# Layer two's output products of five column pairs by Strassen's scheme, with weights streamed from DRAM

## The chip, the cores and the metric

One core of a Trainium2 chip. The metric is device time of one execution in microseconds (us); of several runs the median is given.

## The reference, cut to what is computed

Attention over channels gives a 6016 x 256 matrix, and two layers follow, each a product with a 256 x 2048 matrix, an activation, and a product with a 2048 x 256 matrix. The change touches layer two and the preparation of its weights.

```python
def _moe2_ref(x, w_in, w_out) -> np.ndarray:
    h = x @ w_in
    g = np.maximum(0.01 * h, h)
    return (g @ w_out).astype(np.float32)

def reference(**kwargs):
    ...
    attn_out = _attn_ref(**attn_kwargs)
    B, S, D = attn_out.shape
    x = attn_out.reshape(B * S, D)
    x = _moe_ref(x=x, **moe_kwargs)
    return _moe2_ref(x=x, **moe2_kwargs)
```

## The kernel before

Activations are kept transposed: features on the 128 partitions, tokens along the free axis. The 6016 tokens are taken in six pairs `p` of two blocks `u`, 512 tokens each (448 in the last pair). The 2048 hidden features are taken in eight steps `f`; a step handles feature tiles `f` and `f + 8`. So one step of one pair is, on either side of the activation, a 2 x 2 block product: first weights (2 x 2 tiles of 128 x 128) times inputs (2 x 2 tiles of 128 x 512), then output weights times activated tiles.

Each fp32 product is made of three fp32r matmuls, from a high part and a low part of each operand: high by high, low by high, high by low (`terms`, the helper whose line L92 issues nearly all matmuls). A "product" below is three matmuls of 512 columns. The high part is a cast on ScalarE, the low part a subtraction on VectorE (`halves`, or the two written apart).

In every pair but the very first of layer one, the first 2 x 2 product goes by Strassen's scheme in the Winograd form: seven products instead of eight, in the blocks A11, S2, A12, S3, S1, S4, A22 of combined weights and with the combined inputs B11, T2, B21, T3, T1, B22, T4. `step` issues them into two PSUM banks, h0 (`pa`) and h1 (`pb`). Copies and additions on ScalarE and VectorE between the products, and accumulation on top of what a bank already holds, form the four hidden tiles. The second 2 x 2 product is done plainly: eight products, summed over the steps in the four banks y00, y01, y10, y11 (`put`). So a step is 15 products, 45 matmuls.

The output products of a step lag by about a step. They stand in a list, and `step` takes some of them between its own products, so that TensorE has two products to do while a bank is read by another engine. Two such turnarounds recur. After product S1 into `pa`, VectorE adds it to `tt`, and only then may S4 accumulate into `pa`. After S4, VectorE adds `pa` to `tv`, and only then may the next step's A11 start in `pa`. Engines run their own instructions in the order of the program text; nothing is reordered by a scheduler.

Layer two's weights are prepared in layer one, by a generator `jobs` that `step` advances with `go_on(count)`, a few VectorE instructions at a time: a float64 word is turned to fp32, for the first weights the combined blocks are formed, and high and low parts are stored in DRAM (`w2a`, `w2o`). In layer one's last pair each step reloads weights of layer two, once, into the tiles `wa` and `wo` that layer one no longer needs; there they stay for all of layer two. `prefetch` loads the next pair's inputs and forms their combinations between the products; `switch` forms those that must wait until the pair ends.

Of the kernel before, what the change touches and what calls it, by code (L numbers as in the profile page):

```python
# [7 lines left out]
F32 = mybir.dt.float32  # L8
# [9 lines left out]
def tile_kernel(  # L18
# [28 lines left out]
    nc = tc.nc  # L47
# [35 lines left out]
    w2o = [dram.tile([P, 2, 2, C], F32, name=f"w2o{f}") for f in range(NF)]  # L83
# [30 lines left out]
    with tc.manual_schedule():  # L114
# [26 lines left out]
        def load_piece(key):  # L141
# [3 lines left out]
            if name in ("wi", "w2i"):  # L145
# [55 lines left out]
        def convert(key):  # L201
# [43 lines left out]
            if name == "w2o":  # L245
                w = early.tile([P, 2, BLK], F32R, tag="ws", name="w2o", bufs=2)
                nc.vector.tensor_copy(w[:, 0], flat)
                yield
                subtract(w[:, 1], flat, w[:, 0].bitcast(F32))
                nc.sync.dma_start(  # L250
                    out=w2o[f].rearrange("p h s c -> p h (s c)"), in_=w.bitcast(F32)
                )
                stored.add(key)
                yield
                return
            hi, lo = (
                early.tile([P, 7, P], F32R, tag="ws", name=f"w2a{x}", bufs=2) for x in "hl"
# [4 lines left out]
            yield  # L262
            yield from combine(a)
            nc.vector.tensor_copy(hi[:, 3:], a)
            yield
            subtract(lo[:, 3:], a, hi[:, 3:].bitcast(F32))
            for i, x in enumerate((hi, lo)):
                nc.sync.dma_start(out=w2a[f][:, i], in_=x.bitcast(F32))
# [385 lines left out]
        ys, left = {}, {}  # L654

        def put(item, kc):
# [4 lines left out]
            if key not in ys:  # L661
# [5 lines left out]
            c0 = slice(kc * P, (kc + 1) * P)  # L667
            terms(ys[key][kc][:, :w], (wo[g][:, 0, s, c0], wo[g][:, 1, s, c0]),
                  (gh, gl), first, final)
# [22 lines left out]
        def finish(layer, p, u, kc, y):  # L692
# [10 lines left out]
            if kc == 0:  # L703
                outs[p, u] = early.tile([P, KC, BLK], F32, tag="cv", name="o", bufs=3)
            o = outs[p, u]
            nc.vector.transpose(out=o[:, kc, :w], in_=y)  # L706
            for a in range(P // SB):

                (nc.scalar if p == NPAIR - 1 and a % 2 else nc.sync).dma_start(
                    out=blocks_of(out, p, u, kc, a), in_=blocks_in(o[:, kc, :], p, a)  # L710
                )
# [65 lines left out]
        def reload(f):  # L777

            while ("w2i", f) not in stored:
                go_on(1)  # L780
            pool = early if f < EARLY else late
            wa[f] = pool.tile([P, 2, 7, P], F32R, tag=f"wa{f}", name=f"wa2{f}")
            nc.sync.dma_start(out=wa[f].bitcast(F32), in_=w2a[f])

        def reload_out(f):
            while ("w2o", f) not in stored:
                go_on(1)
            pool = early if f < EARLY else late
            wo[f] = pool.tile([P, 2, 2, C], F32R, tag=f"wo{f}", name=f"wo2{f}")
            nc.sync.dma_start(out=wo[f].bitcast(F32), in_=w2o[f])  # L790
# [69 lines left out]

        def step(layer, p, f):
# [3 lines left out]
            x = xa[p % 2 if layer == 1 else (NPAIR + p) % 2]  # L865
            wf = wa[f]

            def product(dst, a, xs, b, more=False):
                terms(dst, (wf[:, 0, a], wf[:, 1, a]), (xs[:, 0, b, :w], xs[:, 1, b, :w]),
                      not more, True, more)  # L870

            pa, pb = (bank(f"h{i}")[:, :w] for i in range(2))

            def kept(tag):
                return early.tile([P, BLK], F32, tag=tag, name=tag)[:, :w]

            def outputs(count):
                for _ in range(min(count, len(slots))):
                    put(*slots.pop(0))

            tp, tv, tt = (kept(tag) for tag in ("tp", "tv", "tt"))
            product(pa, A11, x, B11)
            nc.scalar.copy(pb, pa)  # L883
            finish_step()
            slots = [(item, kc) for item in pend for kc in range(KC)]
            pend.clear()
            outputs(2)
            product(pb, S2, x, T2, more=True)
            nc.scalar.copy(tv, pb)  # L889
            product(pa, A12, xbt, B21, more=True)  # L890
            act(layer, tp, pa)
            outputs(1)
            product(pb, S3, x, T3, more=True)
            nc.scalar.copy(tt, pb)  # L894
            product(pa, S1, x, T1)
# [9 lines left out]
            outputs(len(slots) - 3)  # L905
            cc = late.tile([P, 2, BLK], F32, tag="cc", name="cc")[:, :, :w]
            product(pa, S4, xbt, B22, more=True)
            add(cc[:, 0], tv, pa)
            product(pb, A22, xbt, T4, more=True)
# [3 lines left out]
            if f:  # L913
                go_on(2)
            fetch()
# [3 lines left out]
            begun.append((layer, p, f, cc))  # L919
            if f < NF - 1:  # L920
                go_on(3)
            fetch()

        def last_step(layer, p, f):
# [3 lines left out]
            x = xa[p % 2 if layer == 1 else (NPAIR + p) % 2]  # L928
            wf = wa[f]

            def product(dst, a, xs, b, more=False):
                terms(dst, (wf[:, 0, a], wf[:, 1, a]), (xs[:, 0, b, :w], xs[:, 1, b, :w]),
                      not more, True, more)
# [7 lines left out]
            nc.scalar.copy(tp, pa)  # L941
            product(pb, S2, x, T2)
            add(tv, tp, pb)
            product(pc, S1, x, T1)
            add(tt, tv, pc)
            product(pd, S3, x, T3)
            add(tt, tt, pd)
# [98 lines left out]
```

## Time and profile before

| | us |
|---|---|
| median of 3 runs | 1036.0 |
| lowest and highest | 1035.88, 1036.09 |
| the profiled execution, its own time | 1036.65 |
| its span, first to last instruction | 1034.9 |
| TensorE (PE) busy | 1027.8 (99%) |
| VectorE (DVE) busy | 625.4 (60%) |
| ScalarE (ACT) busy | 677.0 (65%) |
| granted TensorE clock, share of full | 0.999 |

PEld is TensorE's weight load, which lies beside the matmuls. SP is the engine that issues nearly all DMAs. "Idle before" is the time that an engine stood still just ahead of a group of instructions, and the name behind the arrow is what ended it. A matmul's duration in the trace contains the tail of a pipeline, so the time that one takes from the engine is read from the starts of two groups, not from a duration.

### The profile page before, as it was taken

To read this page: it belongs to the slowest core of one execution; us is meant where nothing else is said; L and a number is where in the kernel's file an instruction comes from. 1 tells how busy PE (TensorE), PEld (TensorE's weight loads), DVE (VectorE), ACT (ScalarE), POOL (GpSimd) and SP (SyncE) were. 2 spreads that over 40 slices of the span, in tenths; PEclk is the share of its full clock that TensorE was granted. 3 is DMA by queue.
4 is the path that set the end of the run, shared out by engine and by line. 5 is a ranking of instruction groups with operands and counts; after the bars stand their busy time and mean duration, and the time that the engine had idled before them with its cause. 6 is when DMAs were issued, how large, how long until landed. Compare 5 with 4: busy or idle time off the path is not lost.

```text
span 1034.9 us, 12664 instructions
## 1 busy us (share of the span) xinstructions
PE 1027.8 (99%) x4664; PEld 868.1 (84%) x4664; DVE 625.4 (60%) x991; ACT 677.0 (65%) x1135; POOL 0.8 (0%) x7
## 2 busy tenths in 40 slices
PE   9999999999999999999999999999999999999998
PEld 7888878888888888888998888888888888888997
DVE  7899865667676767666654445455345455444434
ACT  7675556676676667667666666666666667566664
POOL 0000000000000000000000000000000000000000
PEclk9999999999999999999999999999999999999999
DMA  9765413015125114223644003002101200300202
GB/s 351 249 163 152 134 42 92 10 31 148 56 72 148 69 67 127 85 77 130 238 161 153 1 1 81 2 1 38 43 1 23 60 1 4 74 1 1 42 1 36
DMA packets 124862, 81.83 MB, mean 79 GB/s; under 512 B 97664, under 2 KB 108928, under 8 KB 123520
## 3 DMA queue, kind: packets, MB, share of 16 engines
q1 hardware_dynamic: 120512, 80.04, 26.1%
q10 hardware_dynamic: 4288, 0.98, 0.4%
q8 instruction: 36, 0.59, 0.2%
q14 instruction: 26, 0.21, 0.1%
HBM read 55.05 MB, written 25.95 MB: 78 GB/s over the span
## 4 chain that ended last, share of the span: by engine, by line
PE 98%; DMA 1%; DVE 0%; ACTq 0%; issue 0%; SPq 0%; DVEq 0%
PE y L92 50%; PE h L92 44%; PE y L406 3%; DMA qk<-in_k_dram 1%; PE h L553 1%; PE y L553 0%; ACTq L339 0%; PE y L511 0%; PE h L426 0%; DVE tt L99 0%; DVE o L706 0%; PE h L535 0%; PE h L500 0%; SPq L339 0%; DVEq L99 0%
## 5 line engine op out<-in xcount | busy, mean ns | idle before, releaser
L92 PE MATMUL y<-gd,wo 128*128 128x512 f32 (+1 forms) x1248 | 310.5, 386 | 0.0
L92 PE MATMUL h<-xa,wa 128*128 128x512 f32 (+1 forms) x1152 | 304.6, 386 | 0.0
L92 PE MATMUL y<-g,wo 128*128 128x512 f32 (+1 forms) x1044 | 275.0, 385 | 0.0
L92 PEld LDWEIGHTS y<-gd,wo 128*128 128x128 f32 x1248 | 234.0, 188 | 43.6
L92 PEld LDWEIGHTS h<-xa,wa 128*128 128x128 f32 x1152 | 216.1, 188 | 40.2
L92 PE MATMUL h<-xb,wa 128*128 128x512 f32 (+1 forms) x888 | 231.4, 386 | 0.8 <-DVE tt L99 0.8
L92 PEld LDWEIGHTS y<-g,wo 128*128 128x128 f32 x1044 | 196.1, 188 | 36.2
L92 PEld LDWEIGHTS h<-xb,wa 128*128 128x128 f32 x888 | 166.6, 188 | 32.8 <-DVE tt L99 1.5
L96 DVE TENSOR_TENSOR gd<-cc,gd 128x1024 fp32r<-128x1024 f32 (+1 forms) x87 | 104.4, 1200 | 111.5 <-ACT gd L95 111.3
L99 DVE TENSOR_TENSOR tt<-tt,h 128x512 f32<-128x512 f32 (+1 forms) x88 | 59.4, 675 | 166.0 <-PE h L92 163.6
L883 ACT COPY h<-h 128x512 f32<-128x512 f32 (+1 forms) x87 | 48.8, 561 | 94.1 <-PE h L92 93.4
L99 DVE TENSOR_TENSOR cc<-tv,h 128x512 f32<-128x512 f32 (+1 forms) x89 | 60.0, 675 | 54.4 <-PE h L92 54.3
L894 ACT COPY tt<-h 128x512 f32<-128x512 f32 (+1 forms) x87 | 50.3, 578 | 64.3 <-PE h L92 64.2
L95 ACT CAST gd<-cc 128x1024 fp32r<-128x1024 f32 (+1 forms) x87 | 89.9, 1034 | 0.0
L889 ACT COPY tv<-h 128x512 f32<-128x512 f32 (+1 forms) x87 | 50.3, 578 | 38.4 <-PE h L92 38.4
L99 DVE TENSOR_TENSOR g<-tt,g 128x512 fp32r<-128x512 f32 (+1 forms) x87 | 58.6, 674 | 0.0
L99 DVE TENSOR_TENSOR g<-tp,g 128x512 fp32r<-128x512 f32 (+1 forms) x87 | 58.6, 673 | 0.0
L904 ACT CAST g<-tt 128x512 fp32r<-128x512 f32 (+1 forms) x87 | 53.2, 611 | 2.8
L901 ACT CAST g<-tp 128x512 fp32r<-128x512 f32 (+1 forms) x87 | 53.4, 613 | 0.0
L96 DVE TENSOR_TENSOR xa<-stg,xa 128x512 fp32r<-128x512 f32 (+1 forms) x44 | 29.9, 679 | 28.5 <-ACT xa L95 28.3
L650 ACT ACTIVATE cc<-h 128x512 f32<-128x512 f32 (+1 forms) x47 | 27.8, 591 | 28.8 <-PE h L92 28.7
L406 PE MATMUL y<-qk 128*128 128x256 f32 x188 | 42.9, 386 | 1.1 <-DMA qk<-in_k_dram 1.1
(114 smaller groups left out, 714.3 us busy)
## 6 DMA issues: line engine op xcount, KB each, us to landing
cv<-in_moe_w_in_dram SPq DMA_DIRECT2D x32, 256.0 KB, 3.4
cv<-in_moe_w_out_dram SPq DMA_DIRECT2D x16, 512.0 KB, 3.7
wa<-w2a SPq DMA_DIRECT2D x8, 896.0 KB, 5.3
x<-stg SPq DMA_DIRECT2D x5, 1024.0 KB, 4.3
stg<-x SPq DMA_DIRECT2D x5, 1024.0 KB, 5.4
out_dram<-o SPq DMA_DIRECT2D x80, 64.0 KB, 1.9
qk<-in_q_dram SPq DMA_DIRECT2D x8, 512.0 KB, 10.1
qk<-in_k_dram SPq DMA_DIRECT2D x8, 512.0 KB, 10.2
```

What stands on the lines that cost most here:

```text
L92: nc.tensor.matmul(dst, lhsT=w, rhs=x, start=start, stop=stop, skip_group_check=more)
L95: nc.scalar.copy(hi, raw)
L96: nc.vector.tensor_tensor(out=lo, in0=raw, in1=hi.bitcast(F32), op=ALU.subtract)
L99: nc.vector.tensor_tensor(out=out, in0=in0, in1=in1, op=op)
L406: nc.tensor.matmul(s_ps[h][:, :C], lhsT=t[:, 1, r, h * P:(h + 1) * P], rhs=t[:, 0, r, :], start=(j == 0 and r == 0), stop=(j == last and r ...
L553: nc.tensor.matmul(pw, lhsT=e[:, d, c0], rhs=wi[:, x, d], start=i == 0, stop=i == len(todo) - 1)
L650: nc.scalar.activation(out=out, in_=in_, func=AF.Prelu, alpha=0.01)
L883: nc.scalar.copy(pb, pa)
L889: nc.scalar.copy(tv, pb)
L894: nc.scalar.copy(tt, pb)
L901: nc.scalar.copy(g11[:, 0], tp)
L904: nc.scalar.copy(g22[:, 0], tt)
```

## The change

In the five pairs of layer two that have 512 tokens, the second 2 x 2 product goes by the same scheme. `strassen_step` takes the place of `step`. Its four activated tiles are g[:, 0], g[:, 1], g[:, 2] and `g21`. Differences of them are formed in `first_stage` of the following step (`t13`, `t24`), and six products of combined output weights are summed over the eight steps in six banks: M1 in y00, M3 in y01, M5 in y10, M6 in y11, M7 in h2, M4 in h3. In an ordinary step the products stand in the order A11, M3, M1, S2, A12, M4, S3, S1, M5, M7, S4, A22, M6; the M of a step come in the step after, M4 in the one after that. The seventh product, M2 (weights' A21 with `g21`) is not made in the steps. Its right operand is kept in fp32, four steps to a tile (`keep`), and at the pair's end `begin_drain` issues eight fp32 matmuls of 512 columns, in two bursts of four, onto bank y00 with the fp32 weights `raw2`. Then six additions and four transposes on VectorE, spread over the next pair's steps 0 to 2, make the four output blocks.

The combined weights of a step, first and output side, are 7 blocks x 2 parts each; they don't all fit. `stream_in` and `stream_out` load them from DRAM for each step of each pair, 896 KB each (512 KB on the output side in the last pair), into a ring of six tiles, about a step and a half ahead. Operands live in the tiles of the old `wo`. `prefetch` and `switch` in layer two are replaced by `between` and `beyond`, which place one or two of the same instructions in each step.

The last pair (448 tokens) keeps `step`, and takes the drain of the fifth pair. In layer one, `convert` now makes the combined output weights too (24 pieces of work for the two matrices of a step instead of 16), and `step` calls `go_on(4)` twice instead of `go_on(2)` and `go_on(3)`.

TensorE, from product S1 of a step in layer two to the next A11 (h0 and h1 are `pa` and `pb`; y00 to y11, h2 and h3 hold sums; g0, g1, g2 are operands of high and low parts). Before:

```order
L92 MATMUL h0_5221<-xa0_109,wa27_4702 128x512 x3
L92 MATMUL y01_4818<-g11_5186,wo26_4704 128x512 x3
L92 MATMUL y10_4801<-gd_5230,wo26_4704 128x512 x3
L92 MATMUL h0_5221<-xb_110,wa27_4702 128x512 x3
L92 MATMUL h1_5222<-xb_110,wa27_4702 128x512 x3
L92 MATMUL y11_4802<-gd_5230,wo26_4704 128x512 x3
L92 MATMUL y00_4817<-gd_5230,wo26_4704 128x512 x3
L92 MATMUL y01_4818<-gd_5230,wo26_4704 128x512 x3
L92 MATMUL h0_5296<-xa1_576,wa20_4153 128x512 x3
```

With the change:

```order
L93 MATMUL h0_5926<-xa1_577,wa26_5813 128x512 x3
L93 MATMUL y10_5585<-g1_5936,wo25_5815 128x512 x2
L93 MATMUL y10_5585<-g1_5937,wo25_5815 128x512
L93 MATMUL h2_5589<-g1_5936,wo25_5815 128x512 x2
L93 MATMUL h2_5589<-g1_5937,wo25_5815 128x512
L93 MATMUL h0_5926<-xb_111,wa26_5813 128x512 x3
L93 MATMUL h1_5927<-xb_111,wa26_5813 128x512 x3
L93 MATMUL y11_5603<-g2_5958,wo25_5815 128x512 x2
L93 MATMUL y11_5603<-g2_5959,wo25_5815 128x512
L93 MATMUL h0_6002<-xa1_577,wa27_5891 128x512 x3
```

Two output products still stand between S1 and S4; between S4 and the next A11 there are now two products instead of four.

VectorE, one whole step of layer two in which the next pair's inputs are prepared (xa and stg rows). Before, with the first row of the step after:

```order
L96 TENSOR_TENSOR gd_5086<-cc_5054,gd_5086 128x1024
L99 TENSOR_TENSOR tt_5081<-tt_5081,h0_5077 128x512
L99 TENSOR_TENSOR g11_5114<-tp_5079,g11_5114 128x512
L99 TENSOR_TENSOR cc_5126<-tv_5080,h0_5077 128x512
L99 TENSOR_TENSOR g22_5115<-tt_5081,g22_5115 128x512
L96 TENSOR_TENSOR xa1_576<-stg_4922,xa1_576 128x512
L99 TENSOR_TENSOR stg_4922<-stg_4922 128x512
L96 TENSOR_TENSOR gd_5158<-cc_5126,gd_5158 128x1024
```

With the change, one whole step (the two t24 rows are its two halves):

```order
L100 TENSOR_TENSOR t13_5934<-g_5879 128x1024
L100 TENSOR_TENSOR t24_5935<-g_5879,t13_5934 128x512
L100 TENSOR_TENSOR t24_5935<-keep_5844,t24_5935 128x512
L100 TENSOR_TENSOR g1_5937<-t13_5934,g1_5936 128x1024
L100 TENSOR_TENSOR xa0_110<-stg_5574,xa0_110 128x512
L100 TENSOR_TENSOR stg_5574<-stg_5574 128x512
L100 TENSOR_TENSOR g_5956<-tt_5929,h0_5926 128x512
L100 TENSOR_TENSOR g2_5959<-t24_5935,g2_5958 128x1024
L100 TENSOR_TENSOR g_5956<-tv_5928,h0_5926 128x512
L100 TENSOR_TENSOR g0_5980<-g_5956,g0_5979 128x1024
```

The addition that frees `pa` for S4 (`g<-tt,h0`) now stands behind five or six other VectorE instructions of its step instead of one.

TensorE at the pair's end, the new pair's step 0 from S1 on. Before (the step has the shape of any other):

```order
L92 MATMUL h0_5296<-xa1_576,wa20_4153 128x512 x3
L92 MATMUL y01_4818<-g11_5258,wo27_4787 128x512 x3
L92 MATMUL y10_4801<-gd_5305,wo27_4787 128x512 x3
L92 MATMUL h0_5296<-xb_110,wa20_4153 128x512 x3
L92 MATMUL h1_5297<-xb_110,wa20_4153 128x512 x3
```

With the change:

```order
L93 MATMUL h0_6080<-xa0_110,wa20_5968 128x512 x3
L1095 MATMUL y00_5541<-keep_5512,raw2_4801 128x512 x4
L93 MATMUL y10_5585<-g1_6090,wo27_5970 128x512 x2
L93 MATMUL y10_5585<-g1_6091,wo27_5970 128x512
L93 MATMUL h2_5589<-g1_6090,wo27_5970 128x512 x2
L93 MATMUL h2_5589<-g1_6091,wo27_5970 128x512
L93 MATMUL h0_6080<-xb_111,wa20_5968 128x512 x3
L93 MATMUL y11_5603<-g2_6113,wo27_5970 128x512 x2
L93 MATMUL y11_5603<-g2_6114,wo27_5970 128x512
L1095 MATMUL y00_5541<-keep_5844,raw2_4801 128x512 x4
L93 MATMUL h1_6081<-xb_111,wa20_5968 128x512 x3
```

The two bursts of fp32 matmuls (L1095) stand inside the two turnarounds of that step.

The diff, cut to what the prediction speaks of:

```diff
+            if name == "w2o":
+                nc.vector.tensor_copy(hi[:, 7], a[:, 3])
+                raw = early.tile([P, P], F32, tag="wr", name="wr")
+                nc.vector.tensor_copy(raw, a[:, 1])
+                nc.sync.dma_start(out=w2r[:, f], in_=raw)
+                yield
+                subtract(lo[:, 7], a[:, 3], hi[:, 7].bitcast(F32))
+                yield
             yield from combine(a)
...
+        SLOTS = 6
+
+        def slot(n, shape, name):
+            f = n % SLOTS
+            return (early if f < EARLY else late).tile(shape, F32R, tag=f"wa{f}", name=name)
+
+        def stream_in(k):
+            if k < NPAIR * NF:
+                p, f = divmod(k, NF)
+                while ("w2i", f) not in stored:
+                    go_on(1)
+                iw[p, f] = slot(2 * k, [P, 2, 7, P], f"wa2{f}")
+                nc.sync.dma_start(out=iw[p, f].bitcast(F32), in_=w2a[f])
...
+        def out_product(p, f, m, block, xs):
+            if f == 0:
+                sums[p, m] = bank(m)
+            t = ow[p, f]
+            terms(sums[p, m], (t[:, 0, block], t[:, 1, block]), xs, f == 0, f == NF - 1)
+
+        def strassen_step(p, f):
...
+            product(pa, S1, T1)
+            if f == 0 and drains:
+                drains.pop(0)()
+            add(g[:, 2], tt, pa)
+            act(2, g[:, 2], g[:, 2])
+            g0 = operands("g0")
+            nc.scalar.copy(g0[0], g[:, 0::2])
+            next_stage()
+            beyond(2, p, f)
+            outputs(2)
+            product(pa, S4, B22, more=True)
+            add(g[:, 1], tv, pa)
+            act(2, g[:, 1], g[:, 1])
+            subtract(g0[1], g[:, 0::2], g0[0].bitcast(F32))
...
+            def first_stage():
...
+                subtract(t13, g[:, 1:3], g[:, 0:2])
+                nc.scalar.copy(g1[0], t13)
+                subtract(t24[:, 0], g[:, 2], t13[:, 0])
+                subtract(t24[:, 1], g21, t24[:, 0])
+                subtract(g1[1], t13, g1[0].bitcast(F32))
...
+            def second_stage():
+                g2 = mine["g2"] = operands("g2")
+                nc.scalar.copy(g2[0], mine["t24"])
...
+            def burst(fs):
+                for f in fs:
+                    nc.tensor.matmul(
+                        sums[p, M1], lhsT=raws2[0][:, f], rhs=keep[p, f // 4][:, f % 4],
+                        start=False, stop=True, skip_group_check=True,
+                    )
+
+            def join():
+                burst(range(NF // 2, NF))
+                tc = early.tile([P, BLK], F32, tag="ta", name="c", bufs=2)
+                add(ta, ta, sums[p, M6])
+                add(tb, ta, sums[p, M7])
+                add(ta, ta, sums[p, M5])
+                add(ta, ta, sums[p, M3])
+                add(tc, tb, sums[p, M5])
+                held_out.extend([(1, 0, ta), (1, 1, tc)])
...
+        def between(layer, p, f):
+            if layer == 1:
+                return
+            k = NF * p + f
+            if k >= 1:
+                stream_in(k + 2)
+            if k >= 2:
+                stream_out(k + 1)
...
+            if f == 5:
+                t = staged_x[p]
+                low(x, p, T3, 1)
+                subtract(t[:, 0], t[:, 3], t[:, 0])
+                cast(x, p, T2, 0)
...
+                if layer == 2 and p < NPAIR - 1:
+                    strassen_step(p, f)
+                else:
+                    step(layer, p, f)
```

## Rows read from the trace of the kernel before

**Rows 1.** The page: each engine's busy time, and the chain that ended last

```profile
PE 1027.8 (99%) x4664; PEld 868.1 (84%) x4664; DVE 625.4 (60%) x991; ACT 677.0 (65%) x1135; POOL 0.8 (0%) x7
...
PE y L92 50%; PE h L92 44%; PE y L406 3%; DMA qk<-in_k_dram 1%; PE h L553 1%; PE y L553 0%; ACTq L339 0%; PE y L511 0%; PE h L426 0%; DVE tt L99 0%; DVE o L706 0%; PE h L535 0%; PE h L500 0%; SPq L339 0%; DVEq L99 0%
```

**Rows 2.** Windows: stretch, length, busy of each engine, clock, DMA share, GB/s

```profile
600.00:1000.00 400.00, 400.00 (x1787) 335.39 (x1786) 195.74 (x270) 259.45 (x431) 0.00 (x0) 1.00 0.11 24
```

**Rows 3.** Timeline of TensorE in layer two: start, length, line, tiles, count

```profile
625.39 0.84 PE L92 MATMUL h<-xa,wa 128*128 128x512 f32 x3
...
629.47 1.52 PE L92 MATMUL h<-xa,wa 128*128 128x512 f32 x6
630.83 0.84 PE L92 MATMUL y<-g,wo 128*128 128x512 f32 x3
...
635.59 0.84 PE L92 MATMUL h<-xa,wa 128*128 128x512 f32 x3
```

**Rows 4.** Timeline of TensorE near the start, fp32 matmuls (L406, L500) and fp32r

```profile
12.97 27.43 PE L406 MATMUL y<-qk 128*128 128x256 f32 x126 [0.86 <-DMA qk<-in_k_dram]
```

**Rows 5.** The same timeline, some 30 us later

```profile
42.87 0.61 PE L500 MATMUL h<-ident,rn 128*128 128x128 f32 x4
43.31 2.32 PE L406 MATMUL y<-qk 128*128 128x256 f32 x10
...
50.80 0.94 PE L92 MATMUL h<-xa,wa 128*128 128x512 f32 x3
51.59 0.66 PE L553 MATMUL y<-wi,eth 128*128 128x256 f32 x4
```

**Rows 6.** Timeline of VectorE in layer two

```profile
625.21 1.90 DVE L96 TENSOR_TENSOR xb<-stg,xb 128x512 fp32r<-128x512 f32 x3 [1.05 <-ACT xb L95]
...
631.10 0.69 DVE L99 TENSOR_TENSOR tt<-tt,h 128x512 f32<-128x512 f32 x1 [1.98 <-PE h L92]
...
634.43 2.08 DVE L706 STREAM_TRANSPOSE o<-y 128x512 f32<-128x512 f32 x3
638.09 1.23 DVE L96 TENSOR_TENSOR gd<-cc,gd 128x1024 fp32r<-128x1024 f32 x1 [1.58 <-ACT gd L95]
```

**Rows 7.** Timeline of ScalarE in the same stretch

```profile
624.56 1.65 ACT L95 CAST xb<-stg 128x512 fp32r<-128x512 f32 x3
...
630.35 0.59 ACT L894 COPY tt<-h 128x512 f32<-128x512 f32 x1 [0.76 <-PE h L92]
...
631.82 0.63 ACT L650 ACTIVATE tt<-tt 128x512 f32<-128x512 f32 x1 [0.36 <-DVE tt L99]
632.48 0.62 ACT L904 CAST g<-tt 128x512 fp32r<-128x512 f32 x1
...
637.00 1.05 ACT L95 CAST gd<-cc 128x1024 fp32r<-128x1024 f32 x1
```

**Rows 8.** Groups of VectorE, 600 to 1000 us: busy, mean ns, idle before

```profile
L96 DVE TENSOR_TENSOR gd<-cc,gd 128x1024 fp32r<-128x1024 f32 (+1 forms) x39 | 47.3, 1212 | 76.2 <-ACT gd L95 76.2
L99 DVE TENSOR_TENSOR tt<-tt,h 128x512 f32<-128x512 f32 (+1 forms) x40 | 27.1, 679 | 78.7 <-PE h L92 76.4 <-ACT g L901 2.3
```

**Rows 9.** Timeline of both engines where TensorE waits for VectorE

```profile
151.45 0.69 DVE L99 TENSOR_TENSOR tt<-tt,h 128x512 f32<-128x512 f32 x1 [2.09 <-PE h L92]
...
152.19 1.66 PE L92 MATMUL h<-xb,wa 128*128 128x512 f32 x6 [0.85 <-DVE tt L99]
```

**Rows 10.** Groups of VectorE in layer one, 184 to 500 us

```profile
L99 DVE TENSOR_TENSOR tt<-tt,h 128x512 f32<-128x512 f32 (+1 forms) x31 | 21.1, 681 | 57.3 <-PE h L92 57.3
...
L99 DVE TENSOR_TENSOR w2al<-ta,w2ah 128x384 fp32r<-128x384 f32 (+1 forms) x16 | 10.0, 623 | 0.3
L99 DVE TENSOR_TENSOR ta<-ta 128x128 f32<-128x128 f32 x32 | 9.2, 289 | 0.7
```

**Rows 11.** The DMA view: issues, KB of each, median us to landing

```profile
wa<-w2a SPq DMA_DIRECT2D x8, 896.0 KB, 5.3
...
w2a<-w2ah SPq DMA_DIRECT2D x8, 448.0 KB, 2.5
```

**Rows 12.** Windows (columns as in rows 2): the reload of weights, and the first loads

```profile
505.00:530.00 25.00, 25.00 (x125) 23.19 (x124) 15.09 (x23) 16.80 (x31) 0.00 (x0) 1.00 0.60 211
...
8.00:40.00 32.00, 30.86 (x142) 26.80 (x142) 28.80 (x49) 25.41 (x45) 0.00 (x0) 1.00 0.99 359
```

More of the change, by code (lines that the diff above doesn't have):

```diff
@@ L702, in finish @@
                 return
[L703 to L711, printed above, removed]
+            store(p, u, kc, y)
         def prefetch(layer, p):
@@ L859, in tile_kernel, with kept, products, product @@
                 fetch()
+        def kept(tag, w):
+            return early.tile([P, BLK], F32, tag=tag, name=tag)[:, :w]
+        def products(layer, p, f):
+            w = width[p]
+            x = xa[p % 2 if layer == 1 else (NPAIR + p) % 2]
+            wf = wa[f] if layer == 1 else iw[p, f]
+            def product(dst, a, b, more=False):
+                xs = xbt if a in (A12, S4, A22) else x
+                terms(dst, (wf[:, 0, a], wf[:, 1, a]), (xs[:, 0, b, :w], xs[:, 1, b, :w]),
+                      not more, True, more)
+            return product
@@ L861, in step, with outputs, next_stage @@
+        def outputs(count):
+            for _ in range(min(count, len(slots))):
+                slots.pop(0)()
+        slots, ahead, stages, held_back, drains = [], [], [], [], []
+        def next_stage(some=1):
+            for _ in range(some):
+                if stages:
+                    stages.pop(0)()
         def step(layer, p, f):
             w = width[p]
[L865 to L870, printed above, removed]
@@ L872, in step @@
-            pa, pb = (bank(f"h{i}")[:, :w] for i in range(2))
[L874 to L882, printed above, removed]
+            product = products(layer, p, f)
+            pa, pb = (bank(f"h{i}")[:, :w] for i in range(2))
@@ L883, in step @@
+            tp, tv, tt = (kept(tag, w) for tag in ("tp", "tv", "tt"))
+            product(pa, A11, B11)
             nc.scalar.copy(pb, pa)
-            finish_step()
-            slots = [(item, kc) for item in pend for kc in range(KC)]
+            next_stage()
+            slots.extend(lambda item=item, kc=kc: put(item, kc) for item in pend for kc in range(KC))
             pend.clear()
+            if f == 1:
+                slots[2:2] = held_back
+                held_back.clear()
             outputs(2)
-            product(pb, S2, x, T2, more=True)
+            product(pb, S2, T2, more=True)
@@ L904, in step @@
             nc.scalar.copy(g22[:, 0], tt)
[L905 removed]
+            next_stage()
+            beyond(layer, p, f)
+            outputs(2)
             cc = late.tile([P, 2, BLK], F32, tag="cc", name="cc")[:, :, :w]
[L907 removed]
+            product(pa, S4, B22, more=True)
             add(cc[:, 0], tv, pa)
[L909 removed]
+            if f == 0 and drains:
+                outputs(len(slots))
+                drains.pop(0)()
+            product(pb, A22, T4, more=True)
             act(layer, cc[:, 1], pb)
@@ new lines, in tile_kernel, with store @@
+        rest, held_out, raws2 = [], [], []
+        def store(p, u, kc, y):
+            w = width[p]
+            if (p, u) not in outs:
+                outs[p, u] = early.tile([P, KC, BLK], F32, tag="cv", name="o", bufs=3)
+            o = outs[p, u]
+            nc.vector.transpose(out=o[:, kc, :w], in_=y)
+            for a in range(P // SB):
+                (nc.scalar if p == NPAIR - 1 and a % 2 else nc.sync).dma_start(
+                    out=blocks_of(out, p, u, kc, a), in_=blocks_in(o[:, kc, :], p, a)
+                )
@@ L924, in last_step, with beyond @@
+        def beyond(layer, p, f):
+            if layer == 2 and f == 0:
+                if p:
+                    low(xbt, p, B22, 3)
+                    low(xbt, p, T4, 0)
         def last_step(layer, p, f):
             w = width[p]
[L928 to L933, printed above, removed]
+            product = products(layer, p, f)
@@ L967, in last_step @@
             nc.scalar.copy(g11[:, 0], tp)
-            product(pd, A22, xbt, T4, more=True)
+            product(pd, A22, T4, more=True)
             add(cc[:, 1], tv, pd)
```

262 lines of the change are left out of this document (197 added, 65 removed).

## The prediction

> **What bounds the kernel now.** I read the page's busy times and its chain first: TensorE is busy 1027.8 of 1034.9 us, and the chain that ended last is 98% TensorE, split about evenly between the first and second products of the layers [rows 1]. Then the window over layer two's steps: 400.00 of 400 us busy at full clock, VectorE 195.74, ScalarE 259.45, DMA a share of 0.11 [rows 2]. So no wait of another engine ends last in layer two, and what a step costs is what its matmuls take. A step lasts from one A11 to the next, 625.39 to 635.59: 10.20 us for 45 matmuls, or 0.2267 each; a product is 0.68, as the starts 630.83 and 629.47 (six matmuls apart) also give [rows 3].
>
> **What TensorE loses.** In 5 pairs x 8 steps the second side falls from 24 matmuls to 18: 240 matmuls x 0.2267 = -54.4 us.
>
> **What TensorE gains.** 5 x 8 = 40 fp32 matmuls of 512 columns. The trace has no such matmul. It has fp32 ones of 256 columns, each as two records: 126 records in 27.43 us, of which some 0.16 is the last one's tail, so 0.2164 per record and 0.433 per matmul [rows 4]. Whether that grows with the columns, or is a floor of the weight load, is seen from the 128-column ones: four records from 42.87 to 43.31, 0.11 each [rows 5]. Half the columns, half the time; so 512 columns should take two records of 0.433, 0.866 in all, and 40 of them 34.6 us. Ends: if a record of 512 columns took no more than an fp32r matmul of 512 columns, 2 x 0.2267 x 40 = 18.1; if each were a quarter dearer, 43. I take 34.6, since the three widths lie on a line. Going over from fp32 to fp32r costs something: three fp32r matmuls that followed fp32 ones took 0.79 (50.80 to 51.59) [rows 5] instead of 0.68. Ten bursts x 0.11 = 1.1.
>
> TensorE alone: -54.4 + 34.6 + 1.1 = **-18.7 us**. This is all on the path, as far as nobody makes TensorE wait.
>
> **Whether VectorE and ScalarE keep up.** A step shrinks from 10.20 to 39 x 0.2267 = 8.84 us while VectorE gets more work. Its durations: 0.68 for 512 columns, 1.21 for 1024 [rows 8]. Back to back it is quicker: three of 512 in 1.90, so (1.90 - 0.69) / 2 = 0.605 from start to start; transposes 0.68 [rows 6]. For 1024 I take off the same 0.08: 1.14. One that reads what its predecessor just wrote I count in full. A step with two instructions for the next pair's inputs: t13 1.25 (t24 reads it), t24 0.72 + 0.61, three low parts 3 x 1.14, two additions 1.21, two inputs 1.21: 8.4 of 8.84. It fits, but the order matters, so I walk one such step, A11 starting at 0. Products start every 0.68: M3 and M1 0.68, 1.36; S2 2.04, A12 2.72, M4 3.40, S3 4.08, S1 4.76, M5 and M7 5.44, 6.12, S4 6.80, A22 7.48, M6 8.16. Handing over takes 0.20 from a product's last slot to ScalarE (S3's ends at 630.15, the copy starts at 630.35) and 0.27 to VectorE (630.83, 631.10) [rows 3, 6, 7]; 0.04 from ScalarE to VectorE (638.05, 638.09) and 0.03 back [rows 6, 7]; 0.05 from VectorE to TensorE (152.14, 152.19) [rows 9].
> VectorE: the previous step's second addition starts at 7.75 - 8.84 = -1.09, g0's low part at -0.48, t13 at 0.66, t24 at 1.91 and 2.63, g1's low part 3.24, the inputs 4.38 to 5.59. S1's slots end at 5.44, so the addition that frees `pa` could start at 5.71 and does: VectorE has 0.12 to spare. It ends at 6.40, S4 could start at 6.45 and is due at 6.80.
> ScalarE: copy of `pb` 0.88; g1's cast waits for t13, 1.91 to 2.86; copy to tv 2.92, activation 3.60, g2's cast 4.09, copy to tt 5.04 to 5.63, before VectorE wants it at 5.71. (1.05 per 1024-wide cast, 0.59 per copy, some 0.1 less from start to start [rows 7].) Behind it the activation of g[:, 2] at 6.43, g0's cast 7.09 to 8.14, the other activations 8.47 and 8.99.
> The second turnaround: S4's slots end at 7.48, the addition runs 7.75 to 8.44, A11 is due at 8.84. So both turnarounds keep 0.35 us, and an ordinary step costs no wait.
> Step 0 of a pair has room (two bursts of 3.5 us), but its five additions start after M6 and run until about 0.45 us into step 1. There a transpose, an addition and another transpose join (2.1 instead of 1.21), and the addition for S4 ends at 6.94 instead of 6.40: S4 waits 0.2. I allow 0.3 a pair, **+1.5 us**; bounds 0 and 5 (a step-1 wait of 1 us each).
>
> **Whether the weights arrive.** 1,835,008 bytes per step of 8.84 us is 208 GB/s. They are asked for near 4.1 us of a step, when M4 has let the output tile go, and wanted a step later plus 8.84 - 4.1: 13 us. One such 896 KB load landed in 5.3 us [rows 11]. In the reload of before, 211 GB/s ran at a DMA share of 0.60 with TensorE busy 25.00 of 25; near the start the queues carried 359 [rows 12]. Priced at nothing; that slack hides it. On SP these loads stand behind the stores of output blocks, which wait for transposes of the same step, so they may slip by 1 to 2 us, not by 13.
>
> **Layer one.** Per pair of weight tiles 24 pieces instead of 16, eight per step instead of about five, each 0.29 to 0.69 [rows 10]: some 1.5 us more of VectorE in a step. VectorE there stands idle 57.3 / 31 = 1.85 us a step ahead of the addition for S4 [rows 10]. A weight's high-part cast also waits until the store before it has left its tile (448 KB land in 2.5 us [rows 11]; four pieces fill some 2.3 of that). Eight such places, some 0.1 us each: **+1 us**; bounds 0 and 8.
>
> **Sum.** -18.7 + 1.5 + 1 = -16.2. The profiled execution's own 1036.65 becomes 1020.4; it lies 0.65 above the median of 1036.0, so the median becomes **1019.8 us**; I say 1019.5.
>
> **The rivals.**
> *No stall at all*, and the bursts at two columns' time without a change-over: 1036.0 - 54.4 + 34.6 = 1016.2. For it: every 0.35 above. It is the lower end of the forecast.
> *VectorE becomes the bound of the steps.* If its instructions don't overlap, the step above is 4 x 1.21 + 6 x 0.68 = 8.9 plus hand-overs, say 9.1, in steps 1 to 6 of each pair, and 9.8 in step 1: 5 x (5 x 0.25 + 0.9) = +10.8, so 1030. Against it: 1.90 us for three [rows 6]. For it: those three wait for nothing in between, and here every instruction carries a wait. The Trainium skill (VectorE: DVE Perf Modes, "The DRAIN you can't avoid") says that the next operation doesn't start until the pipeline of the one before is empty; it adds in the same place that one which isn't held starts earlier. By the first half the sum would be this rival's 1030; the three in 1.90 us are with the second half.
> *Layer one stalls.* If the eight places cost 1 us each, 1027.
> *The weights come late* (the other side). One load alone moved 896 KB in 5.3 us [rows 11]. If the two loads of a step don't overlap, a step takes 10.6 us instead of an average of 9.7 with its share of the burst (77.9 / 8): 40 x 0.9 = +36, so 1056. It decides from 180 GB/s down, where a step's loads take the old 10.2 us. Against it: 211 GB/s at a share of 0.60 [rows 12].
>
> **Chances and range.** Forecast with its lower end (1016 to 1023) 0.64; VectorE bound (1023 to 1031) 0.17; layer one (1022 to 1030) 0.09; weights late (1040 to 1060) 0.06; a mix that eats the gain (1032 to 1040) 0.04. The range leaves out the last two and the thin ends: 1015.5 to 1029. A measurement tells 0.2%, about 2.1 us, from no change: faster 0.89, same 0.03, slower 0.08.
>
> **What the new profile would show.** Right: starts of A11 8.84 us apart in steps 1 to 7 of pairs 0 to 4 of layer two; bursts of some 3.5 us; TensorE idle under 5 us in layer two; VectorE over 85% busy there; the DMA share near 0.6 and no wait of TensorE for a weight tile. VectorE as bound: VectorE without idle time, and TensorE idle ahead of S4 or A11 with the releaser DVE. Late weights: TensorE's loads ended by a DMA into wa or wo. Layer one: A11 starts over 10.20 us apart, waiting for VectorE's gd. Wrong in its size without any wait: fp32 records of another length than 0.433.

## The result, and the profile after

The changed kernel took a median of 1025.1 us (four runs, 1024.7 to 1025.75) against 1036.05 for the kernel before, measured beside it: a ratio of 0.989 (0.988 to 0.991). It is 10.9 us faster; 16.5 had been forecast. The profiled execution took 1024.71 us with a span of 1022.9, so between the two profiled executions the gain is 11.94, where the sum of the prediction had 16.2. That miss of 4.3 us is what the rest explains; the other 1.3 us of the difference come from where each profiled execution lies beside its median (0.65 above before, 0.41 below now) and from rounding.

The page after: each engine's busy time and the chain that ended last by line, as in [rows 1], and two kinds of DMA issue, as in [rows 11] (KB of each, median us from issue to landing).

```profile
PE 1013.1 (99%) x4504; PEld 835.3 (82%) x4504; DVE 798.2 (78%) x1213; ACT 711.3 (70%) x1140; POOL 0.8 (0%) x7
...
PE h L93 46%; PE y L93 38%; PE y L413 3%; PE y L1095 3%; DMA stg<-x 3%; DVE g L100 1%; DMA qk<-in_k_dram 1%; PE h L560 1%; ACT g L1027 1%; DVE t L100 1%; ACT g L657 0%; ACT xa L1146 0%; DVE a L100 0%; PE y L560 0%; DVE o L1132 0%
...
stg<-x SPq DMA_DIRECT2D x5, 1024.0 KB, 7.3
out_dram<-o SPq DMA_DIRECT2D x80, 64.0 KB, 3.9
```

TensorE's busy time fell by 14.7 us and is again nearly the whole span. But the chain by line now has 3% of a DMA that was nowhere in the sum: `stg<-x`, the load of the next pair's inputs. The windows over layer one and over layer two (columns as in [rows 2]):

```profile
184.00:500.00 316.00, 316.00 (x1408) 263.67 (x1407) 233.95 (x426) 217.65 (x362) 0.00 (x0) 1.00 0.33 109
600.00:1000.00 400.00, 397.35 (x1695) 316.16 (x1694) 334.02 (x407) 292.23 (x443) 0.00 (x0) 1.00 0.64 202
```

The waits of TensorE and of ScalarE (for whom: us in total, times, longest):

```profile
PE y L93 <- DVE g L100: 2.9, 6, 0.8
PE y L93 <- ACT g L1027: 0.8, 1, 0.8
...
ACT xa L1146 <- DMA stg<-x: 7.2, 4, 2.6
```

Layer one has no wait of TensorE. Layer two has 2.65 idle us in 400, VectorE went from 196 to 334 busy us, and the DMA share is 0.64 at 202 GB/s. No wait for a tile of weights is listed. ScalarE waited four times, 7.2 us in all, for `stg<-x`: once in each of pairs 1 to 4.

**Where the time went, step by step.** A step is again measured from one A11 to the next. Idle times in brackets are reckoned from modelled ends and say less than the starts do. TensorE's timeline over a pair's end (start, length, line, tiles, count):

```profile
617.11 0.84 PE L93 MATMUL h<-xa,wa 128*128 128x512 f32 x3
...
622.61 3.59 PE L1095 MATMUL y<-keep,raw 128*128 128x512 f32 x8
625.64 1.26 PE L93 MATMUL y<-g,wo 128*128 128x512 f32 x3
626.74 0.84 PE L93 MATMUL h<-g,wo 128*128 128x512 f32 x3
...
642.01 0.84 PE L93 MATMUL h<-xa,wa 128*128 128x512 f32 x3
...
650.85 0.84 PE L93 MATMUL h<-xa,wa 128*128 128x512 f32 x3
652.47 0.73 PE L93 MATMUL y<-g,wo 128*128 128x512 f32 x2 [0.78 <-ACT g L1027]
653.73 1.20 PE L93 MATMUL y<-g,wo 128*128 128x512 f32 x4 [0.53 <-DVE g L100]
...
661.61 0.84 PE L93 MATMUL h<-xa,wa 128*128 128x512 f32 x3
```

An ordinary step is 8.84 us (642.01 to 650.85), as forecast to the hundredth. A burst of four fp32 matmuls, eight records, takes 622.61 to 625.64, and the triple behind it 1.10 instead of 0.68: 3.45 in all. The records start 0.43 apart (3.59 less the last one's 0.59, over seven). Steps 0 and 1 of the new pair last 24.90 (617.11 to 642.01) against 2 x 8.84 + 2 x 3.45 = 24.58. And the step from 650.85 lasts 10.76, waiting first for ScalarE's cast, then for VectorE: the step that no term of the prediction had.

| between the two profiled executions | forecast | measured |
|---|---|---|
| 240 matmuls fewer | -54.4 | -54.4 |
| 40 fp32 matmuls with the change-over (10 x 3.45) | +35.7 | +34.5 |
| pairs' ends, 1 to 4 (0.32 each) and 5 (about 0.25) | +1.5 | +1.5 |
| steps after f = 2, pairs 1 to 4: 1.92, 1.22, 0.83, 0.62 | 0 | +4.6 |
| steps 1 and 2 of pair 0 | 0 | +2.5 |
| layer one (layer two's first A11: 543.71, before 544.26) | +1 | -0.55 |
| sum | -16.2 | -11.85 |

The first row is counted from the matmuls left out; the sum closes with the 11.94 of the two executions to 0.1. The two rows forecast at 0 are the miss, +7.1; the others gave 2.7 back.

**The 4.6 us.** SP's timeline in step 1 of the new pair:

```profile
636.19 0.44 SPq L792 DMA_DIRECT2D wa<-w2a  x1
637.22 0.52 SPq L805 DMA_DIRECT2D wo<-w2o  x1
639.24 2.69 SPq L1135 DMA_DIRECT2D out_dram<-o  x4
642.03 3.17 SPq L1143 DMA_DIRECT2D stg<-x  x1
```

ScalarE's in step 2, which the load delays:

```profile
647.04 0.59 ACT L1019 COPY tt<-h 128x512 f32<-128x512 f32 x1
650.19 0.62 ACT L1146 CAST xa<-stg 128x512 fp32r<-128x512 f32 x1 [2.56 <-DMA stg<-x]
650.72 0.62 ACT L657 ACTIVATE g<-g 128x512 f32<-128x512 f32 x1
651.38 1.04 ACT L1027 CAST g<-g 128x1024 fp32r<-128x1024 f32 x1
```

The load stands on SP behind step 1's two weight loads and behind four stores of an output block, which wait for the transposes of that step. It is issued at 642.03, and the chain gives it 8.14 us to land (7.71, 7.29 and 6.75 in pairs 2 to 4). The cast of B11 in step 2 wants it from 647.63 on and waits until 650.19. The cast itself is not urgent, but it stands at the head of ScalarE's queue: behind it are the activation of g[:, 2] and the cast of g0 (VectorE's low part of g0 starts only at 652.45, after 2.08 us of idle time), both on the way to the next step's M3 and M1. So TensorE waits in the step after.

**The 2.5 us of pair 0.** Its step 1 is the first with Strassen output products, and M4, which lags two steps, doesn't exist yet. So it has 36 matmuls, which would take 8.16 us, and took 10.53; step 2 took 8.99. In the list of output products nothing fills M4's place, so M5 and M6 come one place early: their last matmul waits for the low parts of g1 (558.06) and g2 (561.95).

```profile
558.06 0.50 PE L93 MATMUL y<-g,wo 128*128 128x512 f32 x1 [0.30 <-DVE g L100]
...
561.95 0.50 PE L93 MATMUL y<-g,wo 128*128 128x512 f32 x1 [0.83 <-DVE g L100]
```

### The profile page after: what moved, and what is told of

Its sections match the earlier page's. It is cut to its first block, busy times and chain, and to the rows that moved or that the text cites. A ratio compares the mean times of both kernels' runs of the same rounds, so it can differ in the third digit from the quotient of the medians.

```text
span 1022.9 us, 12861 instructions
## 1 busy us (share of the span) xinstructions
PE 1013.1 (99%) x4504; PEld 835.3 (82%) x4504; DVE 798.2 (78%) x1213; ACT 711.3 (70%) x1140; POOL 0.8 (0%) x7
## 4 chain that ended last, share of the span: by engine, by line
PE 92%; DMA 4%; DVE 2%; ACT 1%; issue 0%; ACTq 0%; SPq 0%; DVEq 0%
PE h L93 46%; PE y L93 38%; PE y L413 3%; PE y L1095 3%; DMA stg<-x 3%; DVE g L100 1%; DMA qk<-in_k_dram 1%; PE h L560 1%; ACT g L1027 1%; DVE t L100 1%; ACT g L657 0%; ACT xa L1146 0%; DVE a L100 0%; PE y L560 0%; DVE o L1132 0%
## 5 line engine op out<-in xcount | busy, mean ns | idle before, releaser
L93 PE MATMUL y<-gd,wo 128*128 128x512 f32 (+1 forms) x768 | 188.5, 383 | 0.0
L93 PEld LDWEIGHTS y<-gd,wo 128*128 128x128 f32 x768 | 143.8, 188 | 25.1
L100 DVE TENSOR_TENSOR g<-t,g 128x1024 fp32r<-128x1024 f32 x80 | 97.4, 1217 | 0.0
L97 DVE TENSOR_TENSOR gd<-cc,gd 128x1024 fp32r<-128x1024 f32 (+1 forms) x47 | 55.2, 1175 | 35.6 <-ACT gd L96 35.1
L657 ACT ACTIVATE g<-g 128x512 f32<-128x512 f32 x80 | 50.7, 634 | 32.3 <-DVE g L100 31.3
L93 PE MATMUL h<-g,wo 128*128 128x512 f32 x240 | 67.5, 389 | 0.0
L1053 ACT CAST g<-t 128x1024 fp32r<-128x1024 f32 x40 | 42.1, 1053 | 21.5 <-DVE t L100 21.5
L100 DVE TENSOR_TENSOR g<-g,g 128x1024 fp32r<-128x1024 f32 x40 | 48.9, 1221 | 5.5 <-ACT g L1027 5.2
L93 PEld LDWEIGHTS h<-g,wo 128*128 128x128 f32 x240 | 45.0, 188 | 9.4
L100 DVE TENSOR_TENSOR t<-g 128x1024 f32<-128x1024 f32 x40 | 48.6, 1214 | 0.0
```

Of the source, the lines that this page charges most:

```text
L93: nc.tensor.matmul(dst, lhsT=w, rhs=x, start=start, stop=stop, skip_group_check=more)
L97: nc.vector.tensor_tensor(out=lo, in0=raw, in1=hi.bitcast(F32), op=ALU.subtract)
L100: nc.vector.tensor_tensor(out=out, in0=in0, in1=in1, op=op)
L657: nc.scalar.activation(out=out, in_=in_, func=AF.Prelu, alpha=0.01)
L1053: nc.scalar.copy(g1[0], t13)
```

## The experiments

Theory A: the 4.6 us are the input load's place on SP's queue. Rival B: VectorE, now 84% busy, is the bound, and the late load only shows it. Rival C: the streamed weights slow what shares queues with them. Each is followed by its runs. Where only one time stands, it is that of a single execution.

### The input load first (theory A)

```diff
             k = NF * p + f
+            if f == 1 and p < NPAIR - 1:
+                move_in(p + 1)
             if k >= 1:
                 stream_in(k + 2)
...
-            if f == 1:
-                move_in(p)
```

> Edit: in step 1 of each pair of layer two the load of the next pair's inputs (x2, 1 MB, move_in) is issued first on SP, ahead of that step's two weight loads and of the four stores of an output block; in the changed kernel it stands behind them all. Theory A (the load lands only 6.8 to 8.1 us after its issue, the cast of B11 in step 2 waits for it at the head of ScalarE's queue, 0.6 to 2.6 us, and everything behind that cast comes late): in pairs 1 to 4 step 3 goes back from 10.76, 10.06, 9.67 and 9.46 us to 8.84 to 8.9, ScalarE's wait for stg is gone, and the time falls by 4 to 5 us against the changed kernel's 1025.1, to 1020 to 1021. Rival B (the cast isn't what TensorE waits for; step 3 is long because of ScalarE's and VectorE's own work): step 3 stays above 9.4 us and the time stays within 1 us of 1025. Rival C (the weight loads, now behind 1 MB more, come late themselves): TensorE waits for a DMA into wa or wo in step 3, time at or above 1025.

1020.84 us (1019.53 to 1021.05), 0.985 of before (0.983 to 0.987), so 4.3 less than the changed kernel. The load is issued at 636.73 and lands in 5.6 us (median); all the steps that took 9.46 to 10.76 take 8.84, and TensorE is busy without a gap over the four pairs' ends. SP's timeline,

```profile
636.73 0.46 SPq L1143 DMA_DIRECT2D stg<-x  x1
637.28 0.39 SPq L792 DMA_DIRECT2D wa<-w2a  x1
```

and the window over the pairs' ends:

```profile
600.00:940.00 340.00, 340.00 (x1431) 267.22 (x1430) 308.69 (x369) 262.40 (x387) 0.00 (x0) 1.00 0.66 212
```

Theory A holds, and B falls for these steps: VectorE did the same work with the wait gone.

### The input load between the weights and the stores

```diff
+            if f == 1 and p < NPAIR - 1:
+                move_in(p + 1)
             if rest:
                 rest.pop(0)()
...
-            if f == 1:
-                move_in(p)
```

> Edit: the same load is issued behind the step's two weight loads but ahead of the four stores of an output block. It tells what in front of the load makes it late. If it is the stores (65536 bytes each, in 128-byte pieces, and SP takes 2.7 us to issue four): it lands within 6 us of its issue as in the kernel before (5.4), the cast in step 2 doesn't wait, and step 3 is 8.84 to 8.9 in pairs 1 to 4, as with the load put first. If it is the weight loads (1.8 MB ahead of it on the same 16 engines, some 5 us): ScalarE still waits in step 2, by 0.5 us or more, and step 3 keeps at least half of its 0.6 to 1.9 us.

1020.47 us; all the steps that took 9.46 to 10.76 take 8.84. That is what I expected if the stores were the cause, but I also expected the load to land within 6 us of its issue, and it did not. Issued behind two weight loads at 638.13, it took a median of 8.5 us, longer than in the changed kernel. SP's timeline:

```profile
636.50 0.45 SPq L792 DMA_DIRECT2D wa<-w2a  x1
637.52 0.52 SPq L805 DMA_DIRECT2D wo<-w2o  x1
638.13 0.55 SPq L1143 DMA_DIRECT2D stg<-x  x1
639.55 4.25 SPq L1135 DMA_DIRECT2D out_dram<-o  x4
```

It is in time all the same, since it starts 3.9 us earlier. So there are two delays, the wait behind the stores and the company of weight loads, and the next run takes the second one away alone.

### No streaming (rival C)

```diff
         def stream_in(k):
             if k < NPAIR * NF:
                 p, f = divmod(k, NF)
+                if k >= 3:
+                    iw[p, f] = iw[divmod(k - 3, NF)]
+                    return
...
```

(and the same in `stream_out`)

> Left out: all weight loads of layer two but the first three on each side; every later step uses the tiles that are already there, so it computes with other weights. The load of x2 and the stores stay. If the traffic of the weights as such delays the load of x2: the load lands in about 5.4 us as before, ScalarE doesn't wait in step 2, step 3 is 8.84. If the stores alone delay it: it still lands above 6.5 us and step 3 stays above 9.2 in pairs 1 to 4. In either case the other steps show whether streaming costs anything by itself: I expect none (8.84 with and without), and 24.9 us for steps 0 and 1 of a pair together.

1019.86 us. The load is issued even later, at 642.76, still behind the stores, but lands in 5.2 us; ScalarE waits for it once, 0.5 us, and all these steps take 8.84. The pairs' ends keep 24.91 to 24.97. So either cure suffices, an earlier issue or no other traffic; and apart from the input load the streaming costs TensorE nothing that these runs show: with it and the load first the time was 1020.84, 1 us more, within what layer one varies (layer two's first A11 lay between 543.3 and 544.3 in these runs).

### An empty place in pair 0

```diff
-                slots.extend(late_one)
+                slots.extend(late_one or [lambda: None])
```

> Edit: in step 1 of pair 0, where there is no M4 of an older step to fill its place in TensorE's order, the place is left empty instead of being filled by the next product, so that M5, M7 and M6 stand where they stand in every other step. Theory: in the changed kernel that step takes 10.53 instead of 8.84 us since M5 waits 0.30 us for g1's low part and M6 0.83 us for g2's low part, each one place too early; with the gap step 1 takes 9.0 to 9.3 us (38 or so of its matmul slots, S3 waiting 0.1 us for the copy of pb), 1 to 1.5 us off the total. Rival (the step is long because the copies of layer one's last outputs stand on VectorE and ScalarE ahead of t13): it stays above 10 us.

1023.39 us. Pair 0's steps 1 and 2 went from 10.53 and 8.99 to 8.92 and 8.84, 1.76 us less; the waits for the input load stayed (10.37, 9.26, 9.68 and 10.43). Of the 2.5 us of pair 0 some 0.76 remain, as 36 matmuls would take 8.16.

### Both

The two edits above together, the load first and the empty place.

> Edit: both changes together, the load of x2 first on SP in step 1 and the empty place in step 1 of pair 0. If the two waits are independent, their gains add: 4.3 us (the load first: 1025.1 to 1020.8) and 1.75 us (steps 1 and 2 of pair 0: 17.76 instead of 19.52), so 1019 +- 0.7, with all of steps 1 to 7 at 8.84 to 9.0 and 24.9 for steps 0 and 1 together. If the gap only moves work that the load's wait had hidden: above 1020.

1018.72 us (1017.97 to 1019.5), 0.983 of before (0.982 to 0.985): 6.4 less than the changed kernel, and below both edits alone; the steps show the two gains side by side (pair 0's steps 1 and 2 at 8.92 and 8.84, the steps behind the input load at 8.84). Over the pairs' ends (the same window) nothing waits, and VectorE's share is 91%:

```profile
600.00:940.00 340.00, 340.00 (x1429) 266.87 (x1428) 308.09 (x370) 261.17 (x384) 0.00 (x0) 1.00 0.66 210
```

### One more VectorE instruction (rival B)

On top of the last kernel, one addition of 512 columns whose result nobody reads, in each Strassen step ahead of product S1:

```diff
+            add(kept("tp", BLK), g[:, 0], g[:, 0])
```

> Edit, on top of the kernel with both changes: one more VectorE addition of 512 columns (0.605 us from start to start; its result is used by nobody) in every Strassen step of layer two, ahead of the addition that frees pa for S4. Theory (what VectorE has to spare is 0.12 us at that addition and 0.35 at the turnaround, whatever its idle time is elsewhere): in steps 3 to 6 VectorE then needs 8.42 + 0.6 = 9.02 us, so these steps come to 9.0 to 9.1, step 2 to 9.1 to 9.3, step 7 stays at 8.84, steps 0 and 1 together grow by 0.4 to 0.7; in all 6 to 9 us. Rival (VectorE's idle time of 8 to 9% of the stretch, some 0.8 us a step, is there to be used): all steps stay at 8.84 and the time within 1 us.

1030.55 us, 11.8 more; I had expected 6 to 9. The steps from 2 to 6 of pairs 1 to 4, and from 3 to 6 of pair 0, took 9.06 to 9.36 instead of 8.84, step 7 still 8.84, pairs' ends 25.5 instead of 24.9. VectorE's timeline of one such step, from one t13 (`t<-g`) to the next:

```profile
662.31 1.22 DVE L100 TENSOR_TENSOR t<-g 128x1024 f32<-128x1024 f32 x1
663.57 0.69 DVE L100 TENSOR_TENSOR t<-g,t 128x512 f32<-128x512 f32 x1
664.36 0.69 DVE L100 TENSOR_TENSOR t<-keep,t 128x512 f32<-128x512 f32 x1
...
667.31 0.68 DVE L100 TENSOR_TENSOR tp<-g 128x512 f32<-128x512 f32 x1
667.91 0.68 DVE L100 TENSOR_TENSOR g<-tt,h 128x512 f32<-128x512 f32 x1
668.51 1.22 DVE L100 TENSOR_TENSOR g<-t,g 128x1024 fp32r<-128x1024 f32 x1
669.65 0.69 DVE L100 TENSOR_TENSOR g<-tv,h 128x512 f32<-128x512 f32 x1
670.38 1.23 DVE L100 TENSOR_TENSOR g<-g,g 128x1024 fp32r<-128x1024 f32 x1
671.52 1.22 DVE L100 TENSOR_TENSOR t<-g 128x1024 f32<-128x1024 f32 x1
```

No idle time is marked: the step is 9.21 us of VectorE, 0.60 of it the added instruction (667.31 to 667.91). So the changed kernel's step needs 8.6 of VectorE's 8.84, not the 8.42 of my walk. Two hand-overs that I took for 0.605 or 0.72 are longer: the second half of t24 starts 0.79 after the first, which it reads, and 669.65 to 670.38 is 0.73, because g0's low part waits for ScalarE's cast. VectorE is thus not the bound of the changed kernel, but only 0.24 us a step away from it, and a mean of 9% idle over the pairs could not hold an instruction of 0.6.

### Streaming alone

`plain = True` in `stream_out`, and the plain output products in all pairs:

```diff
-                if layer == 2 and p < NPAIR - 1:
-                    strassen_step(p, f)
-                else:
-                    step(layer, p, f)
+                step(layer, p, f)
```

> Edit: the streamed weights alone. All six pairs of layer two take the plain output products (the old step), with weights loaded for every step as in the changed kernel; no fp32 bursts. Theory (streaming costs nothing by itself, and the waits for the load of x2 hurt only where ScalarE is nearly full): steps of 10.20 us throughout layer two and 1035 to 1036.5, the time of the kernel before, even if that load still lands later than 6 us. Rival (streaming, or the other order of the input preparation, costs TensorE something): steps above 10.25 or waits of TensorE for wa or wo, and a time above 1037.

1041.98 us; I had expected the time of the kernel before. Ordinary steps are 10.20 as there, but step 0 of pairs 1 to 4 takes 11.58 to 11.60. In TensorE's timeline B22 and T4 wait for VectorE,

```profile
632.71 1.21 PE L93 MATMUL h<-xb,wa 128*128 128x512 f32 x4 [1.07 <-DVE xb L100]
```

and in VectorE's the low parts of their inputs come late:

```profile
631.97 1.29 DVE L100 TENSOR_TENSOR xb<-stg,xb 128x512 fp32r<-128x512 f32 x2
```

The low parts of B22 and T4 can only be made when the old pair has let their tile go, and `beyond` puts them right ahead of their product; the kernel before made them in `switch`, between the pairs (from 625.21 on [rows 6]), and no wait followed. The changed kernel has the same order as this run, but a burst of 3.45 us stands there and hides it. The traffic itself again costs nothing. ScalarE waited for the input load here too, 6.5 us in four waits:

```profile
653.59 0.62 ACT L1146 CAST xa<-stg 128x512 fp32r<-128x512 f32 x1 [2.04 <-DMA stg<-x]
```

The steps behind it still took 10.20 to 10.23: a step of that length has the room that one of 8.84 lacks.

### No bursts

```diff
-                for f in fs:
+                for f in fs[:0]:
```

> Left out: the eight fp32 matmuls at each pair's end, so one term of one output block is missing; all else is as in the changed kernel. Theory: they cost what the trace shows, 3.45 us for each of ten bursts, so 34.5 us less, 1025.1 - 34.5 = 990.6, if nothing takes their place. Rival: the bursts also hide the five additions of join and the preparation of the new pair's inputs on VectorE; without them TensorE waits for VectorE in steps 0 and 1, 3.3 us of additions of which little else hides, so only 18 to 27 us less, 998 to 1007, and steps 0 and 1 together take 19 to 21 us instead of 17.7.

1019.73 us. This was the widest miss of all: 34.5 us of TensorE's work are gone, and by the profiled executions the time fell by 5.0. The pairs' ends went from 24.90 to 24.35, 24.49, 23.78 and 24.14, and from 25.32 to 25.76 in the last: 2.4 us together. The rest is the late input load, which now held up one step by 0.84 instead of four by 4.6. (The last pair's steps took some 1 us more together, 9.30 instead of 9.12 each; why stays open.) TensorE's timeline at the first pair's end:

```profile
626.15 0.51 PE L93 MATMUL h<-xb,wa 128*128 128x512 f32 x1 [0.94 <-DVE xb L100]
...
631.38 0.93 PE L93 MATMUL y<-g,wo 128*128 128x512 f32 x3 [2.66 <-issue]
632.56 1.65 PE L93 MATMUL y<-g,wo 128*128 128x512 f32 x3 [0.25 <-DVE o L1132]
634.01 1.48 PE L93 MATMUL h<-xa,wa 128*128 128x512 f32 x3
```

VectorE's, the additions of the drain and its first transpose:

```profile
628.43 0.68 DVE L100 TENSOR_TENSOR a<-a,y 128x512 f32<-128x512 f32 x1
...
629.87 1.41 DVE L100 TENSOR_TENSOR a<-a,y 128x512 f32<-128x512 f32 x2
631.20 0.68 DVE L100 TENSOR_TENSOR c<-b,y 128x512 f32<-128x512 f32 x1
631.80 0.71 DVE L1132 STREAM_TRANSPOSE o<-y 128x512 f32<-128x512 f32 x1
```

And the window right behind TensorE's wait:

```profile
633.00:634.00 1.00, 1.00 (x3) 0.72 (x3) 0.96 (x2) 0.35 (x1) 0.00 (x0) 0.50 0.40 70
```

VectorE runs the additions of the drain one behind the other from 628.43 to 631.88. The new pair's M3 goes into y01, which the fourth of them reads (it ends at 631.28), and starts at 631.38; M1 waits for the transpose that empties y00. Behind these waits the granted clock is 0.50, the 1.2 GHz level, and two triples take 1.45 (632.56 to 634.01) and 1.28 instead of 0.68. So at a pair's end VectorE would be the bound if the bursts weren't there, and cheaper bursts alone would bring far less than their length. How much they would bring without the lower clock can't be read here. It cost 1.4 us in these two triples (1.45 + 1.28 - 2 x 0.68); over each of the first four pairs' ends, windows of 23 to 25 us, the granted clock is 0.93, which by estimate is some 1.7 us an end (0.07 x 24).

## Why the prediction was off, step by step

The median of 1025.1 lies inside the stated range of 1015.5 to 1029, but outside the band that held the forecast (1016 to 1023). It lies in the bands of two rivals, VectorE as the bound and layer one, and neither came about. That the range holds it is luck as far as the 7.1 us go for which the sum had no term. Of the signs named for being right, TensorE's idle time (2.65 us), the bursts and the DMA share came true; VectorE stayed at 84% instead of over 85, and steps of 8.84 did not hold in step 1 of a pair (9.11), in the step after f = 2 or at the start of pair 0.

- **TensorE's sum was right.** 39 matmuls at 0.2267 gave 8.84 for a step, measured 8.84. The fp32 record, extrapolated from 128 and 256 columns to 0.433, measured 0.43. A burst took 3.45, forecast 3.57 with its change-over: eight records alone make 3.44, so the change-over of 0.11 did not show. What I didn't see: VectorE's work at a pair's end takes almost as long as the bursts, so that leaving them out brought 2.4 us there and not 34.5 (1019.73).
- **VectorE's walk was right in its verdict, short by 0.2 in its size.** Forecast 8.42, about 8.6 measured. On the rival "VectorE becomes the bound", independent instructions start 0.60 us apart though one lasts 0.68 (667.31, 667.91, 668.51), and one that reads its predecessor's result starts 0.79 after it (663.57, 664.36). The Trainium skill (VectorE: DVE Perf Modes, "The DRAIN you can't avoid") says that the next operation waits for an empty pipeline and that one which isn't held starts earlier; these rows bear out the second half, as [rows 6] did.
- **Pairs' ends** were forecast at 0.3 and took 0.32: right, by the walk of step 1. The forecast for S4 there was a wait of 0.2, and step 1 took 9.11 instead of 8.84.
- **Weights** were forecast to arrive in time, and did: no wait for them, at a share of 0.64 and 202 GB/s.
- **Layer one** was forecast at +1 and cost nothing; it has no wait of TensorE. The 0.55 it gained is within its variation.
- **The step that failed** is the paragraph on whether the weights arrive, together with the walk of ScalarE. The paragraph walked SP's queue for the weights, which have 13 us of slack, and said that the stores ahead of them might cost 1 to 2 us. The input load was issued from the same queue, in the same `between`, behind the same stores, with only 5.6 us until its reader (642.03 to 647.63), and it was not walked at all. The walk of ScalarE goes from the copy to tt (5.04 to 5.63) straight to the activation of g[:, 2] (6.43) and leaves out the reader, the input cast that stands between them. Together they cost 4.6 us by the steps, 4.3 by the run that moves the load. In the kernel before, the same load stood late in step 1 as well, behind 16 stores:

```profile
633.13 9.24 SPq L709 DMA_DIRECT2D out_dram<-o  x16
642.48 0.43 SPq L747 DMA_DIRECT2D stg<-x  x1
```

Its reader came two steps later:

```profile
665.36 0.61 ACT L95 CAST xa<-stg 128x512 fp32r<-128x512 f32 x1
```

The load landed 5.2 us after its issue (647.63) and had 17.7 us to spare. Two things changed: the new order puts the reader 5.6 us behind the issue instead of 22.9, at the head of ScalarE's queue and ahead of the activation that TensorE wants, and weight loads are now in flight beside the load. A later place for the reader was not tried.

- The second miss, **pair 0**, came from walking an ordinary step and the pair's end but not the first step, where M4 is missing: 2.5 us, 1.76 of them curable by one empty place in the list.
- The rivals as written didn't come about. Their idle times were looked for ahead of S4 and A11; the waits stood ahead of M1, M3, M5 and M6.

## What to carry to other kernels

When work is moved onto a queue that runs in order, walk every entry of that queue and not only the new ones: what stands ahead of it and waits for what, when its reader wants it, and what is queued behind that reader. Walk the first and the last round of a lagged schedule too, since an item that is missing there shifts the others. Mean idle time is no measure of room: 9% of VectorE's time was idle and an instruction of 0.6 us cost about 0.36 a step, while leaving out ten bursts worth 34.5 us of TensorE brought 2.4 us at their places, because another engine needed most of that time anyway (and the clock fell behind the waits). When the order of instructions is changed, compare how long each load had before its first reader, before and after.

## What the runs showed of the hardware

- A DMA issue on SP is not always short. The input load took SP 0.43 us in the kernel before and without streaming, but 3.17 behind the stores with streaming; with the load moved ahead, the weight load in that place took 3.27 (644.50 in the first experiment). The Trainium skill (DMA: Bandwidth & Descriptors, "Issuing engines are not separate DMA queues") says that starting a DMA usually takes little beside the DMA itself; 3.17 of the 8.14 us to landing differs from that. Why the issue takes so long there wasn't tried. A long landing does not need it: behind issues of 0.55 us (the second experiment) and 0.91 (streaming alone) the load still took a median of 8.5 and 7.8 us, and 5.2 without streaming.
- The 64 KB stores landed in a median of 3.9 us in the changed kernel and 1.9 without streaming. No engine is listed as waiting for one to land; what they held up is SP's queue, as the input load shows.
- In the run without bursts, where TensorE stood still for 2.66 us (0.94 some five us before), the granted clock afterwards was 0.50 in the window shown and the one behind it, and 1.00 again from 636 on. By the granted clock of 0.93 the next three pairs' ends went the same way.
